# DeltaNet and MLP-mixer on one core: the joins of 16-blocks with block-diagonal operands over the whole array, and a new instruction order

## The chip, the cores and the metric

The kernel runs on one core of a Trainium2 chip. The metric is the device time of one execution in microseconds (us); the kernel before takes 701.34 us, the median of three runs between 700.79 and 702.61. TensorE (PE) does matmuls out of SBUF into PSUM; VectorE (DVE), ScalarE (ACT) and GpSimd (POOL) work element by element; SyncE (SP) issues all the DMAs here. Each engine takes its instructions in the order of its own queue, and waits where an operand isn't there yet.

## The reference

Two blocks follow each other: a delta-rule attention (4 sequences, 8 heads, 768 steps, 48 features) and an MLP-mixer on its output (width 384, token mixing of 256, channel mixing of 1536).

```python
k_n = k / (np.linalg.norm(k, axis=-1, keepdims=True) + 1e-06)
state = np.zeros((B, H, D, D))
for t in range(S):
    kt, vt, bt = k_n[:, :, t], v[:, :, t], beta[:, :, t, None]
    y[:, :, t] = np.einsum('bhd,bhde->bhe', q[:, :, t], state)
    v_old = np.einsum('bhde,bhd->bhe', state, kt)
    state = state + bt[:, :, :, None] * np.einsum('bhd,bhe->bhde', kt, vt - v_old)

x = y.transpose(0, 2, 1, 3).reshape(B, S, H * D)
h = np.maximum(x.transpose(0, 2, 1) @ w_tok1, 0.0) @ w_tok2
u = x + h.transpose(0, 2, 1)
out = u + np.maximum(u @ w_ch1, 0.0) @ w_ch2
```

All arithmetic is float32; the four weight matrices come in as float64 and are rounded to float32 on the chip.

## The kernel before

**Units.** A sequence is cut into 12 chunks of 64 steps; two neighbouring chunks of all 8 heads are a *unit* of 128 steps, so a sequence has 6 units and the batch 24. Unit u's keys and queries are loaded (`load_kq`, job k), transposed and multiplied with one another (`prep`, job p). That yields for every chunk and head a strictly triangular 64x64 matrix, whose entries couple a step to the earlier ones. Its inverse (of the identity plus it) turns the step-by-step rule into a few matmuls per chunk. Both lie in the array `gm`: 8 pairs (`nb`) along the free dimension, 128 partitions.

**The inverse, in blocks.** A 64x64 block is cut into 32x32 diagonal blocks, four per unit and `nb` (`quarters`). The diagonal blocks are inverted by VectorE for a whole *round* of units at once (`invert`, job i), with one block per partition, by repeated multiply (L553) and add (L558). Rounds hold units 0 to 3, 4 and 5, then four units each. The blocks get there and back in two ways:

- The first batch (units 0 to 5, rounds 0 and 1) stays in SBUF: four copies per unit (`to_parts`, L501), a VectorE transpose (L545), and four copies back (`from_parts`, L520). The four copies go to ScalarE, VectorE, ScalarE and GpSimd. Here only the 16x16 halves of each 32-block are inverted on VectorE, and `join_16` (job h, L579 on) makes the off-diagonal 16x16 part of each 32-block: p_z = block x its second inverted half (transposed in `t16`), L587; a scaled copy of it into `z16`, L591; p_x = z x block, L599; four copies into the block. `low16` is 1 on the rows of the second half of each 32-block and 0 elsewhere.
- The later units go through DRAM (`n_dram`, `w_dram`) and have all 32 columns inverted on VectorE, in 30 steps.

`join` (job j) then makes the 32x32 part of each 64-block in the same way: a VectorE transpose into `t11` (L614), p_z (L619), copies into `zst`, p_x (L628), copies back.

In the 16-block join every matmul works on a 32x32 tile of TensorE, four tiles for each of the 8 `nb`:

```python
for nb in range(NB):
    for i, (block, _, _) in enumerate(quarters(u)):
        r = slice(HB * i, HB * i + HB)
        nc.tensor.matmul(p_z[r, nb], block[:, nb], t16[r, :, j * NB + nb])
```

**The recurrence.** Job r walks the chunks of all heads, each step needing the state of the step before: p_k or p_q, p_w, p_s and, in the first batch (`recur_early`), p_y, with copies and subtractions on ScalarE and VectorE between. A recurrence step of unit u needs that unit's join. After the 12 chunks of a batch, `mixer` (job m) does token mixing (p_1, L887; p_h, L900) and channel mixing (p_ut, L910; p_c, L973; p_o, L992) and stores the output. The last pair of rows of the last batch stores its second row block in two halves (L1023, L1031).

**Weights.** 34 pieces are loaded as 64-bit words and rounded (`round_weights`, job w), on ScalarE, VectorE and GpSimd. Pieces w22 to w33 are those of `wc2` (`round_pair`); w24 and w25 lie in its second block `wc2[:, 1]`.

**The order.** Nothing is scheduled while the kernel runs or is built: every job is a Python generator that issues some instructions and yields. A string of words, 2,142 steps long, says which job is advanced when, and with it the order of every engine's queue:

```python
for word in order.split():
    name, _, n = word.partition("*")
    for _ in range(int(n or 1)):
        next(jobs[name])
```

Words x, z and Y issue matmuls on zeros whose result isn't used (`keep_warm` with one or four banks, `warm_tiles`); m0 to m3 are the mixers.

Of the kernel before, what the change touches and what calls it, by code (L numbers as in the profile page):

```python
# [13 lines left out]
C = 64  # L14
U = 128
DP = 64
HB = 32
QB = 16
# [5 lines left out]
def kernel(  # L24
# [70 lines left out]
    def ps_prep(shape, name):  # L95
        return psum.tile(shape, FP32, name=name, tag="prep", bufs=2)
# [176 lines left out]
    def round_pair(j, src):  # L273

        m, k = divmod(j, 2)
        b = wc2[:, m]
        yield from round_weights(
            b[:, 2 * k : 2 * k + 2].rearrange("p j n -> p (j n)"), src, (id(wc2), j)
        )
        if k == 0:  # L280
            return
        assert (id(wc2), j - 1) in rounded
        for out, x, y in ((4, 1, 0), (1, 3, 1), (5, 3, 4), (6, 2, 5)):
            nc.vector.tensor_tensor(
                out=b[:, out], in0=b[:, x], in1=b[:, y], op=ALU.subtract
            )
            rounded.add((id(wc2), m, "sum", out))
            if out != 4:
                yield
# [19 lines left out]
    joined_16 = set()  # L309
    joined = set()  # L310
# [153 lines left out]
    z16 = spare[:, cuts[2] : cuts[3]].rearrange("s (b t) -> s b t", t=QB)  # L464
# [30 lines left out]
    def to_parts(u):  # L495
        rnd, j = round_of[u]
        if u < NCH:
            t = turned_of(rnd)
            for i, (block, at_t, _) in enumerate(quarters(u)):
                on = (nc.scalar.copy, nc.vector.tensor_copy, nc.scalar.copy, nc.gpsimd.tensor_copy)[i]  # L500
# [13 lines left out]
    def from_parts(u):  # L514
        rnd, j = round_of[u]
        assert rnd in turned_back
        if u < NCH:
            for i, (block, at_t, _) in enumerate(quarters(u)):
                on = (nc.scalar.copy, nc.vector.tensor_copy, nc.scalar.copy, nc.gpsimd.tensor_copy)[i]
# [57 lines left out]
    def join_16(u):  # L577
# [17 lines left out]
        for nb in range(NB):
            for i, (block, _, _) in enumerate(quarters(u)):
                r = slice(HB * i, HB * i + HB)
                nc.tensor.matmul(
                    p_x[HB * i : HB * i + QB, nb], z[r, nb], block[:, nb, QB:HB]  # L599
                )  # L600
        yield
        for i, (block, _, _) in enumerate(quarters(u)):
            on = nc.vector.tensor_copy if i in EARLY_DVE else nc.scalar.copy
            on(out=block[0:QB, :, QB:HB], in_=p_x[HB * i : HB * i + QB])
# [275 lines left out]
    def mixer(b):  # L880
# [39 lines left out]
        def store(c, e=slice(0, DM)):  # L920
            nc.sync.dma_start(out=out[b, c * 128 : (c + 1) * 128, e], in_=xb[:, c, e])
# [21 lines left out]
        for c in range(0, NCH, 2):  # L943
# [77 lines left out]
            final = (b, c) == (B - 1, NCH - 2)  # L1021
            if final:
                store(c + 1, slice(DH, DM))  # L1023
# [7 lines left out]
            store(c + 1, slice(0, DH) if final else slice(0, DM))  # L1031
# [33 lines left out]
    w10 z x*2 w10*2 k0 x z b w2 w1 k0 w10 k0*3 w10 k0 x p0 w2*2 p0 b*2 p0 x k1 w2 w1  # L1065
    p0*3 w2 k2 p0 w1 k3 p0*2 k1 z p0*2 z k1*2 p0 w3 k2 k1*2 p1*2 p0 v0*2 k2 k4*2 k2
    p1*2 k2*2 p1*6 k3 p2 w3 k3*2 p2 k3*2 k4*3 w3 p1*3 p2*3 p3*2 k6 p2 k5 p2*3 p3*3
    p2*4 p0 p4*2 k5 p3*3 p1 p3*3 w1*2 p3 p2 p3 p1 p2*2 p0 p4 k4 p0 w3 p2 p3*3 p1*2
    p4*2 p3 p0 k6*2 z w6 k6*2 p4*4 x i0 w3 i0 k6 w18 k5*4 p4 i0*3 w6 i0 w18 i0 p5
    i0*4 v0 p4*2 i0*3 w18 i0*2 p4*2 w18 w6 w13 k8 p5 i0 h0*2 p6 h1 k8 h1 w6 p5 w6  # L1070
    f0*2 v0 v1 v0 p4 k7*2 f1 k7 f1*2 f0*2 f1 w13 h2*2 h0 k7*3 z p6 w18 w13 p6 h0*4
    p7 j0*2 w8*2 h1 p5 w13*2 w8 f2*3 j0 h1*3 p7 w8 h1 Y j1 p6 w11*2 w8 w11 j0 p5 j0
    p5*4 r0*2 w17 f2 w17 h2*2 r0 h2*3 w11 v1 w17 p7 p4*2 p5 r0 p5*3 v1*2 r1*2 k8 r0
    Y w17*2 p5 w11 w14*2 r1 k8 r1 h3 p5*3 r1*2 r0 f3*2 j1*2 h3 f3 i1 r1*2 f3 v1 i1
    k9*4 w0 v2*4 p6 w14 r2 i1 j2 p6*5 j1*2 r2 r1 i1 p7 r2*3 w0 j2*2 i1 w14 w0 r2 i1
    h3*2 r2*2 w0 v2 h3*3 k9 k8 k9 i1 r3*2 k10 i1*2 p6*2 j3 i1 k8 p6 r3 w0 r3*2 j2
    r3*3 w14 p7 p8 p7 j2 p7 k10*2 r4*2 i1 v3 w9*2 p7*3 r4*3 i1 j3*2 v3 w9*2 r4 j3 i1
    j3 r4 w5*2 r2 r5 p6 r4*2 p6*2 w9 i1 p8 p6 k10*2 r5 w5*2 i1 p7*3 k11 v3 r5*3 p8*2
    w5 k10 k11 r5*3 p8*2 i1 p8*2 r5 v3*2 w16 v4 w16 r6*3 w16 w24*2 i1 w27 v4 p7 v4
    p7 h5*2 r6*2 w16 h4 w16 p7 r6*2 p8*2 w27 v4 w24 p9 h4 f4*4 r6*2 r7*2 p9 w24 w27  # L1080
    p9 p10 w24 p8 w27 p8*2 w27 r7*4 f5 p7 k12 w28*2 p9*7 w28 r7*3 v5*2 h4*4 w26 z
    w29 h4 p8 p9 v5*2 w26 f5*2 w26 f5 p9*2 r3 v4 w26 h5*2 z j4 h5*3 w28 k13 p8 w26
    w29 p8 j4*2 w29 r8 p8 w28 w29 k12 j4 v5 p9*2 j4 j5 r8 z p9 r8 p10*3 r8*2 p9 j5
    w7*3 w29 r8*3 i2*3 p10 j5*3 w7 r9*2 w15*2 i2 r9*3 k13 w7 w15*2 i2 r9*4 k12*2 w4
    i2 k12 w4 i2 r8 w4 w15 p12 r10*2 i2*2 w19*2 p10 k11*2 r10*4 i2 w19 v6 w4*2 k11*2
    r10*2 i2 w19*2 w22 k12 i2 r10 r11*3 m0 i2 r11*2 w22 i2 v6 m0 w12 k13*2 w12 i2
    w22 w31 i2 v6 i2*2 w12 i2*3 w12 v7 k13 v7*3 r11*2 i2*2 w12 i2 w21 w22*2 i2 w25
    i2 v6*2 i2*6 m0*2 p10*5 f6 m0*3 p12 m0 f6 m0 w27 m0*2 p10 m0 f6*2 w31 m0*2 f8
    w21*2 r12 v7 w21 Y w31 j6 w21 f7*3 w20 f7 f8*2 j6 w25*2 p10 j7 j6 w25*3 p11*2
    w20*2 f8 w23 w31 w27 w20 w31 w27 w20 m0*2 j7 j6*2 w23*2 p11 p12 m0 p10*3 j8 m0*2  # L1090
    f9*3 p10 k13 r12*2 w23*2 j7 m0 r12*2 j8 m0 j7*2 r13*2 m0 w23 p11 p12 p13 j8
    w32*2 p11 r13*2 w32 p11 m0 p13 r13*2 p13 w32*2 p11*4 m0 r14*2 p11 m0 w29*2 v8*2
    r14 w30 p11*2 j8 w23 w25 r14 p12 w30*2 r14 w23 r14 m0 w30 j8 w30 w25 k14 r15*2
    p13 p12 p11 p12*3 m0 v8*2 p12 v8 r15*2 p12 m0*2 w33*2 f9 p11*2 r15 p12*2 r15 w33
    m0 w29 p13*5 m0 p11 v9 w33 r16*2 j9 k14*4 k15 p12*4 p13*2 v9*2 p13*6 w33*2 m0*2
    w33*2 w31 v9 w31 j9 r16 p14*2 m0*3 r16*3 j9 p14 m0 w31 p14*2 r17*2 m0 v9 j9*2
    k14 i3 r17*2 i3*2 m0 i3 k15 v10 p14*4 k15 v10 i3 v10 i3 k16 v10 i3 k15*2 m0*2
    i3*2 r17*2 m0*2 r18 k15 i3*4 m0*3 i3 p14 r18 i3*3 k16*3 m0 i3*2 k16*2 i3*13
    r18*2 p15 p14*2 m0 p14*2 r18*2 m0*5 f10 v10 m0*7 f10*3 m0 r19 f11*2 r19 p14 p15
    f11 j10 m0 p15 m0*3 r19*2 j10*2 f13*4 f12 p15*2 m0 r19*2 j10 m0 p15 p16 f12 r20  # L1100
    v11 p14 f11 j10 p15*4 r20 m0 j11 f12 r20*2 k17*2 p15*2 k17 v11 f12 v11*3 p14
    p15*2 m0 p15 r20 p15 r20 j11 j12 m0 r21 j11*3 r21 j12 r21*2 m0 s*2 p16*5 j12 p16
    k17*2 v12 k18 m0 v12 m0 p17 j13 r21*2 p16*3 m0 r22 p17 r22 k18 k17 p17 v12 p16*4
    m0 s p17 r22*2 m0 r22 p16 r22 p16*2 m0 r23*2 p17*2 p15 m0*2 v13 m0*2 r23 p17*2
    m0 r23 v12 r23 v12 r23 k19 p17*3 m0*3 v13*2 k18*4 p17*5 m0*2 p17 j13 m0 j12 i4*2
    m0*3 i4*3 m0 i4 m0 i4 v13 m0*2 i4*2 k19 m0*2 k19*2 i4*2 m0 i4 p18 i4 m0*3 k19
    i4*2 j12 j13 m0 k19 j13 i4*2 r24*2 m1 i4 r24*3 m1*2 i4 r25 i4*2 p18*2 r25 i4*3
    v14*2 i4 j13 m1 i4 m1 r25 v13 m1 r25*3 m1 p18 r26*2 i4 m1 v14 i4 v14 i4 p18 i4
    p18 k20 r26 m1 i4*2 r26*3 m1 p19 v14 p18*4 m1 f14 s r27*2 p18*3 f14*2 k20*2 m1*3
    r27*2 p19*2 m1*2 j14 f15*2 f14 f16 f15*2 m1 r27*2 j14*2 m1*2 j15 r28*2 j14 f16  # L1110
    j14 j15*2 k20 f16 p18*2 m1 f17*2 k20 r28*2 p19 j16 m1 p20 r28 j16 r28 j15*2
    r29*2 p20 j16 m1 p19*4 r29 p19 k20 m1 p20 r29*2 p19 v15 p19 f17 r29 v15*4 m1*2
    r30*2 p18 f16 m1*4 r30*2 v16 k21 v16 p18 k21 p19 k21*3 p19 p21 m1 p21 m1*2 v16
    r30 v16*2 p20*4 r30 p20*3 m1 p21 k21 p19*3 r31*2 p20*2 k22*3 p20*3 f17 p20 m1*2
    k22 j16 k22 r31 m1*3 j16 r31 j17 m1 r31*2 v17*2 p20 p21*2 v17 p21*3 m1 r32*2 m1
    p21 m1*2 r32*2 p21 p19 k22 v17 p22 p21*3 p22*2 m1 r32*2 m1 p21*4 p22*2 m1*2
    r33*2 m1 j17 r33*2 k23 m1 k23 i5*3 v17 m1*2 i5*4 v18 k23*2 v18*3 r33 k23*2 r33
    p22 j17*3 i5 m1 p23 m1*3 i5*2 m1 i5 m1 i5 r34 i5*2 m1 r34 m1*7 r34*2 m1 i5 p22
    m1*4 i5 r34*2 m1 i5 m1 i5 m1*2 v18 p22 i5*3 m1*5 r35 m1*6 i5*3 m1*3 i5*2 m1 i5*2
    m1*2 i5*4 p23*2 m1 f18*3 r35 m1 f19 m1 p22*2 f19 f20 f19 f20*3 m1*2 r35*2 p22*3  # L1120
    m1*2 p23 j18 p23 p22*2 m1 p23 f18 m1*5 j18*2 m1*3 p23 m1*2 r35 j19*2 j18 p22 f19
    m1 v19*3 j19 m1*2 p22 m1*6 f21*4 m1*2 j18 m1 p23 m1*2 v19 m1*6 r35 r36*2 p23*4
    r36*3 m2 p23 j20 r37 j20 j19 v19 p23 r37*3 p23*3 v20 m2 j21 r37*2 j20 m2 v20 r38
# [45 lines left out]
```

## Time and profile before

| what | value |
|---|---|
| median of three runs | 701.34 us |
| the profiled execution, its own time | 703.88 us |
| its span, first to last instruction | 702.1 us |
| TensorE busy | 660.9 us (94%) |
| VectorE busy | 476.5 us (68%) |
| ScalarE busy | 279.7 us (40%) |
| GpSimd busy | 105.9 us (15%) |
| mean granted TensorE clock | 0.944 of full speed |

The profile is of one execution. Its page has the engines' busy time, the span in 40 slices, the DMA queues, the chain that ended last (followed back from the last instruction, at each step to what released it), and the costliest groups of instructions. A group is named by the line of the code, the engine, and output<-inputs. The granted clock is the speed at which TensorE was allowed to run, as a share of full speed. Ends of matmuls are modelled, so "busy" on PE is not PE at its peak. Every float32 matmul of the code shows as two instructions in the counts.

### The profile page before, as it was taken

Reading aid. Unit: us, or ns where it says so; the run is one execution under the profiler, and the core shown is the slowest. Engines: PE = TensorE matmul, PEld = TensorE weight load, DVE = VectorE, ACT = ScalarE, POOL = GpSimd, SP = SyncE. Lnnn points to the kernel's source line nnn. Section 1 sums busy time; section 2 is a strip of 40 time slices with the busy share of each in tenths; the row PEclk is TensorE's granted clock in tenths of the full one; section 3 lists DMA queues with packets and bytes.
Section 4 is the critical chain, followed back from the end, with each engine's and each line's share of the span. In section 5 each row is a group of like instructions: output and inputs, shape, how many; then the busy total and the mean of one; then the engine's idle time right before and its main releaser. Section 6 shows DMA issues by size and latency. Waiting matters only on the chain.

```text
span 702.1 us, 18867 instructions
## 1 busy us (share of the span) xinstructions
PE 660.9 (94%) x7794; PEld 594.8 (85%) x7794; DVE 476.5 (68%) x1263; ACT 279.7 (40%) x659; POOL 105.9 (15%) x130
## 2 busy tenths in 40 slices
PE   8448988798999999999999999999999999999998
PEld 5337885656999999987999999977999996999998
DVE  6998787898899955499577895358955533252433
ACT  7647476424642233312743414233424231142230
POOL 2336234225231011101112000000000000000000
PEclk9856689599999999999999999999999999999999
DMA  9844656635254233412444104020020000000000
GB/s 183 168 91 112 112 142 149 166 85 110 65 95 111 60 63 74 86 38 62 76 70 94 41 1 95 8 56 15 13 54 14 1 23 1 22 2 23 1 23 23
DMA packets 146901, 46.15 MB, mean 66 GB/s; under 512 B 138080, under 2 KB 141280, under 8 KB 146816
## 3 DMA queue, kind: packets, MB, share of 16 engines
q1 hardware_dynamic: 146816, 44.95, 29.9%
q8 instruction: 61, 1.00, 0.6%
q14 instruction: 24, 0.20, 0.1%
HBM read 35.49 MB, written 9.44 MB: 64 GB/s over the span
## 4 chain that ended last, share of the span: by engine, by line
PE 83%; DVE 11%; DMA 2%; issue 2%; ACT 2%; SPq 0%; ACTq 0%; DVEq 0%
PE p_o L992 24%; PE p_r L818 7%; PE p_c L973 7%; PE p_c L818 7%; PE p_d L818 5%; PE p_q L730 4%; PE p_s L756 4%; PE p_w L746 4%; PE p_h L900 3%; PE p L887 3%; PE p_g L436 3%; PE p_z L619 2%; PE p_x L628 2%; DVE sub L553 2%; DVE x L558 2%
## 5 line engine op out<-in xcount | busy, mean ns | idle before, releaser
L992 PE MATMUL p_o<-wc,r 128*128 128x192 f32 x720 | 126.0, 328 | 0.6 <-ACT u_t L914 0.6
L992 PEld LDWEIGHTS p_o<-wc,r 128*128 128x128 f32 x720 | 116.4, 190 | 1.8 <-ACT u_t L914 1.1
L918 DVE TENSOR_TENSOR xb<-xb,p_o 128x192 f32<-128x192 f32 x84 | 29.5, 352 | 57.0 <-PE p_o L992 56.6
L558 DVE TENSOR_TENSOR x<-x,sub 128x84 f32<-128x84 f32 (+24 forms) x178 | 59.8, 336 | 6.1
L553 DVE TENSOR_TENSOR sub<-x 128x84 f32<-128x84 f32 (+24 forms) x178 | 58.1, 326 | 7.6 <-DMA x<-n_dram 3.9
L973 PE MATMUL p_c<-u_t,wc 128*128 128x256 f32 x216 | 52.1, 392 | 0.0
L835 DVE TENSOR_TENSOR r<-p_r,r 128x384 f32<-128x384 f32 x36 | 20.0, 555 | 46.1 <-ACT r L864 35.6
L992 PE MATMUL p_o<-wc,s 128*128 128x192 f32 x288 | 50.7, 327 | 0.0
L264 POOL TENSOR_TENSOR w_f<-w_f,d 128x384 uint32<-128x384 uint32 (+1 forms) x34 | 34.2, 1008 | 94.9 <-DVE w_f L257 50.1
L838 ACT ACTIVATE r<-r 128x384 f32<-128x384 f32 x72 | 37.5, 524 | 23.6 <-DVE r L835 21.5
L992 PEld LDWEIGHTS p_o<-wc,s 128*128 128x128 f32 x288 | 46.8, 190 | 0.0
L749 ACT COPY rw_bd<-p_w 64x192 f32<-64x192 f32 x72 | 22.4, 311 | 59.1 <-PE p_w L746 53.6
L973 PEld LDWEIGHTS p_c<-u_t,wc 128*128 128x128 f32 x216 | 40.6, 194 | 5.8 <-issue 0.7
L818 PE MATMUL p_r<-u_t,wc 128*128 128x128 f32 x324 | 45.4, 276 | 0.0
L818 PE MATMUL p_c<-u_t,wc 128*128 128x128 f32 x324 | 45.2, 276 | 0.0
L358 POOL TENSOR_TENSOR v_st<-v_st,nrm 128x384 f32<-128x384 f32 x24 | 20.2, 845 | 165.3 <-DMA v_st<-in_v_dram 116.4
L818 PEld LDWEIGHTS p_r<-u_t,wc 128*128 128x128 f32 x324 | 40.8, 192 | 0.1
L818 PEld LDWEIGHTS p_c<-u_t,wc 128*128 128x128 f32 x324 | 40.5, 192 | 0.2 <-issue 0.2
L415 POOL TENSOR_TENSOR mb<-mask_c,cs 128x512 f32<-128x512 f32 x20 | 21.2, 1059 | 128.9 <-DVE cs L397 113.2
L436 PE MATMUL p_g<-kqt 64*64 64x128 f32 x704 | 29.4, 299 | 7.4 <-ACT kqt L425 5.9
L887 PE MATMUL p<-xb,w 128*128 128x384 f32 x96 | 35.5, 509 | 0.0
L730 PEld LDWEIGHTS p_q<-s_bd,kqt 128*128 128x128 f32 x264 | 33.3, 192 | 2.1 <-issue 0.5
(185 smaller groups left out, 1283.4 us busy)
## 6 DMA issues: line engine op xcount, KB each, us to landing
d<-in_moe_w_ch_dram SPq DMA_DIRECT2D x24, 384.0 KB, 3.7
v_st<-in_v_dram SPq DMA_DIRECT2D x96, 48.0 KB, 2.7
out_dram<-xb SPq DMA_DIRECT2D x23, 192.0 KB, 1.9
kpad<-in_k_dram SPq DMA_DIRECT2D x18, 192.0 KB, 3.9
qpad<-in_q_dram SPq DMA_DIRECT2D x18, 192.0 KB, 3.6
kst<-in_k_dram SPq DMA_DIRECT2D x64, 48.0 KB, 2.9
n_dram<-gm SPq DMA_DIRECT2D x72, 32.0 KB, 1.9
gm<-w_dram SPq DMA_DIRECT2D x72, 32.0 KB, 2.0
```

Of the source, the lines that this page charges most:

```text
L264: nc.gpsimd.tensor_tensor(out=f, in0=f, in1=lo, op=ALU.add)
L436: nc.tensor.matmul(p_g[cc][PAR[i ^ cc], p], kqt[PAR[i], 2 * p + cc, 0], kqt[PAR[i], 2 * p + cc],)
L553: nc.vector.tensor_tensor(out=tmp, in0=y[:, :, 0:s, s : s + 1].to_broadcast([n, k, s, w]), in1=y[:, :, s : s + 1, s + 1 : m].to_broadcast( ...
L558: nc.vector.tensor_tensor(out=y[:, :, 0:s, s + 1 : m], in0=y[:, :, 0:s, s + 1 : m], in1=tmp, op=ALU.add,)
L730: nc.tensor.matmul(p_q[:, p], kqt[:, 2 * p + cc], s0[:, p])
L746: nc.tensor.matmul(p_w[0 : C + 1, p], gm[:, 2 * p + cc, 0 : C + 1], r_bd[:, p])
L818: nc.tensor.matmul(p[:, i], weight(g * n + i), b_, start=first and i == 0, stop=True, skip_group_check=True,)
L838: nc.scalar.activation(out, out, ACTF.Relu)
L887: nc.tensor.matmul(p_1[dh], piece_of(w1, c, 0)[:, dh * 128 : (dh + 1) * 128], xb[:, c], start=(c == 0), stop=(c == NCH - 1),)
L918: nc.vector.tensor_tensor(out=xb[:, c, e], in0=xb[:, c, e], in1=p, op=ALU.add)
L973: nc.tensor.matmul(p_c[:, k], piece_of(wc1, cb, f * 128)[:, f * 128 : (f + 1) * 128], u_t[:, cb], start=(cb == 0), stop=(cb == NCB - 1),)
L992: nc.tensor.matmul(p, a[:, m], wc2[:, m, j], start=(start and m == 0), stop=(m == NM - 1), skip_group_check=True,)
```

## The change

- **Operands.** `z16` goes. Two zeroed operands come: `t16_bd` in its place (128 x 512) and `z16_bd` (128 x 1024), which lies in `wc2[:, 1]` until the weights come there. Both are zeroed by GpSimd. An assertion holds the rounding of w24 and w25 back until all six units have used them.
- **join_16.** Four ScalarE copies put the unit's four 16-column blocks of `t16` on a block diagonal. p_z is then one matmul per `nb` with the unit's whole 128 x 64 stationary operand, and 64 moving columns. Four scaled activations, in place of one, put its diagonal blocks into `z16_bd`. p_x is one matmul per `nb` with 128 stationary and 32 moving columns. The final four copies stay.
- **Block copies.** In `to_parts` and `from_parts` the fourth copy goes from GpSimd to VectorE; `EARLY_DVE` is (1, 3).
- **Last store.** The output's last row block is stored in one piece.
- **Order.** The string of words is new throughout. Each job h has 8 words in place of 7; z, x and Y occur 17, 11 and 2 times in place of 9, 6 and 3.

```diff
@@ round_pair
-        yield from round_weights(
+        late = range(NCH) if m == 1 else ()
+        for n, _ in enumerate(round_weights(
             b[:, 2 * k : 2 * k + 2].rearrange("p j n -> p (j n)"), src, (id(wc2), j)
-        )
+        )):
+            yield
+            assert n != 3 or used_16.issuperset(late)
@@ operands
     t16 = spare[:, cuts[1] : cuts[2]].rearrange("s (t b) -> s t b", t=QB)
-    z16 = spare[:, cuts[2] : cuts[3]].rearrange("s (b t) -> s b t", t=QB)
+    t16_bd = spare[:, cuts[2] : cuts[3]].rearrange("s (b i t) -> s b i t", i=4, t=QB)
+    z16_bd = wc2[:, 1].rearrange("s j n -> s (j n)")[:, 0 : NB * 4 * HB].rearrange(
+        "s (b i t) -> s b i t", i=4, t=HB
+    )
+    for t_ in (t16_bd, z16_bd):
+        nc.gpsimd.memset(t_, 0.0)
@@ to_parts and from_parts, the same line in both
-                on = (nc.scalar.copy, nc.vector.tensor_copy, nc.scalar.copy, nc.gpsimd.tensor_copy)[i]
+                on = nc.vector.tensor_copy if i in EARLY_DVE else nc.scalar.copy
@@ join_16
-        z = z16[:, bs]
-        p_z = ps_prep([128, NB, QB], "p_z")
+        wt = gm_of(u)
+        rows = [slice(HB * i, HB * i + HB) for i in range(4)]
+        for i, r in enumerate(rows):
+            nc.scalar.copy(t16_bd[r, :, i], t16[r, :, bs].rearrange("s t b -> s b t"))
+        yield
+        taken_16.add(u)
+        p_z = ps_prep([128, NB, 4 * QB], "p_z")
         for nb in range(NB):
-            for i, (block, _, _) in enumerate(quarters(u)):
-                r = slice(HB * i, HB * i + HB)
-                nc.tensor.matmul(p_z[r, nb], block[:, nb], t16[r, :, j * NB + nb])
-        taken_16.add(u)
-        yield
-        nc.scalar.activation(z, p_z, ACTF.Copy, scale=low16)
+            nc.tensor.matmul(
+                p_z[0:C, nb], wt[:, nb, 0:C], t16_bd[:, nb].rearrange("s i t -> s (i t)")
+            )
+        yield
+        for i, r in enumerate(rows):
+            r2 = rows[i % 2]
+            nc.scalar.activation(
+                z16_bd[r, :, i, 0:QB], p_z[r2, :, QB * i : QB * i + QB],
+                ACTF.Copy, scale=low16[r2],
+            )
         yield
         assert inverted.issuperset((u, i) for i in range(4))
-        p_x = ps_prep([128, NB, QB], "p_x")
+        p_x = ps_prep([128, NB, 2, QB], "p_x")
         for nb in range(NB):
-            for i, (block, _, _) in enumerate(quarters(u)):
-                r = slice(HB * i, HB * i + HB)
-                nc.tensor.matmul(
-                    p_x[HB * i : HB * i + QB, nb], z[r, nb], block[:, nb, QB:HB]
-                )
+            nc.tensor.matmul(
+                p_x[:, nb], z16_bd[:, nb].rearrange("s i t -> s (i t)"),
+                wt[:, nb, 0:C].rearrange("s (two t) -> s two t", two=2)[:, :, QB:HB],
+            )
+        used_16.add(u)
         yield
         for i, (block, _, _) in enumerate(quarters(u)):
             on = nc.vector.tensor_copy if i in EARLY_DVE else nc.scalar.copy
-            on(out=block[0:QB, :, QB:HB], in_=p_x[HB * i : HB * i + QB])
+            on(out=block[0:QB, :, QB:HB], in_=p_x[HB * i : HB * i + QB, :, i % 2])
@@ mixer, the last stores
-            final = (b, c) == (B - 1, NCH - 2)
-            if final:
-                store(c + 1, slice(DH, DM))
...
-            store(c + 1, slice(0, DH) if final else slice(0, DM))
+            store(c + 1)
@@ the order: all lines replaced; here those around the third inversion's end
-    i2 v6*2 i2*6 m0*2 p10*5 f6 m0*3 p12 m0 f6 m0 w27 m0*2 p10 m0 f6*2 w31 m0*2 f8
-    w21*2 r12 v7 w21 Y w31 j6 w21 f7*3 w20 f7 f8*2 j6 w25*2 p10 j7 j6 w25*3 p11*2
-    w20*2 f8 w23 w31 w27 w20 w31 w27 w20 m0*2 j7 j6*2 w23*2 p11 p12 m0 p10*3 j8 m0*2
+    v6*3 i2 k11 w12 k13 v6 w31*2 i2*2 w24*2 i2*2 w24 i2*3 w31 p10*4 r11 m0*2 p10 r11
+    w24 x w24 w31*2 w12*2 m0*3 v6 p12 p10 w25 w12*2 w21 r12 w25*2 z f6*3 p12*2 p10
+    w20 f6 w25 j6*2 w25 p11 w21*2 z j6 f7*3 w20 w21 j6*2 j7 w20 j7*2 w21 p11 w20
+    w23*3 r12*2 w23 p11 w20 f9 w23 p11*2 p12*2 r12 w29 m0 r12 m0*2 p11 m0 w25 w23*2
```

## The prediction

> **What bounds the kernel now.** I read the page first: engine busy times, the slices, the chain by line. Then busy time by stage, the chain in order of time, and the engines' timelines where a stage changes hands.
>
> ```profile
> PE 660.9 (94%) x7794; PEld 594.8 (85%) x7794; DVE 476.5 (68%) x1263; ACT 279.7 (40%) x659; POOL 105.9 (15%) x130
> PEclk9856689599999999999999999999999999999999
> ```
>
> Averaged, TensorE is the bound; the clock digits say that the first quarter is another regime. Busy time by stage (columns: busy us and instructions of PE, weight load, VectorE, ScalarE, GpSimd, then granted clock, DMA share, GB/s) shows where it ends:
>
> ```profile
> 29.30:42.40 13.10, 1.99 (x32) 1.58 (x32) 12.28 (x39) 1.68 (x4) 3.30 (x4) 0.51 0.72 131
> 56.60:98.00 41.40, 37.55 (x993) 33.80 (x992) 32.66 (x92) 23.50 (x60) 15.72 (x18) 0.71 0.56 115
> 125.40:156.60 31.20, 27.16 (x264) 18.45 (x264) 29.00 (x85) 11.40 (x27) 6.02 (x8) 0.73 0.47 114
> 164.30:698.50 534.20, 533.54 (x5132) 497.00 (x5133) 337.64 (x886) 186.36 (x434) 47.51 (x54) 1.00 0.21 45
> ```
>
> From 164.3 us on PE idles 0.7 us in 534: the end is "when the saturated part begins" plus "what PE still has to do then". Before it, VectorE bounds the first and second inversions and the third one (125.4 to 156.6), and PE, largely at half clock, the recurrence steps between. The chain in order of time (start, duration, step) shows the hand-over:
>
> ```profile
> 115.65 2.98 DMA n_dram<-gm
> 118.82 6.61 DMA x<-n_dram
> ...
> 156.41 0.21 DVE x L558
> ```
>
> PE's timeline there (start, duration, group, in brackets the idle time before it and its releaser):
>
> ```profile
> 152.14 4.48 PE L900 MATMUL p_h<-r,w 128*128 128x384 f32 x12
> 157.15 4.14 PE L900 MATMUL p_h<-r,w 128*128 128x384 f32 x12 [0.52 <-DVE xb L904]
> 161.12 0.82 PE L910 MATMUL p_ut<-ident,xb 128*128 128x128 f32 x6
> 164.35 0.69 PE L619 MATMUL p_z<-t,gm 32*32 32x32 f32 x32 [1.82 <-DVE t L614]
> ```
>
> The last unit of the third inversion is sent out at 115, its 30 steps run on VectorE to 156.6, its result goes through DRAM, and the join of unit 6 (p_z of L619) starts at 164.35. While it waits for that, PE does p_h and p_ut of the first mixer.
>
> **What the skill says.** The Trainium skill, "TensorE: Matmul & The Clock Gate", Part 2 (Step-by-step): weight-load time scales with the columns, not the rows. The trace agrees: 8 passes (four matmuls, two records each) of p_s (112 columns) hold PE 0.77 us and 8 of p_q (128 columns) 0.87 us in the chain, 0.096 and 0.109 us a pass at the same 96 moving columns. The Trainium skill, "TensorEngine Tiling (Array Packing)", The Solution: 32x32 tiles run independently. Agrees: the 64 passes of a p_z of the 16-block join take 0.66 us (98.06 to the next group at 98.72), 10 ns each. The Trainium skill, "TensorE: Matmul & The Clock Gate", Part 1: the clock is halved until PE has been busy for a window of about 3.4 us. The trace shows halved stretches (0.51 in the table's first row) but also 0.5 from 77 to 94 us with PE busy on small tiles, so busy time alone doesn't lift it. The Trainium skill, "GPSIMD Engine Reference", section 8, Key points: GpSimd shares its SBUF interfaces with VectorE and can contend with it. Agrees: the VectorE copy of L501 takes 367 ns alone and 858 beside a GpSimd copy.
>
> **The change, part by part.** Six units, each with one 16-block join. Queue positions are those of the two built programs.
>
> *PE, the joins.* Removed per unit: 64 passes of p_z (0.62 us by cadence) and 64 of p_x (0.62). Added: 8 matmuls, 16 passes, for p_z with 64 columns and 64 moving; at the 0.87 ns per column of the rows above 0.056 us, so 0.90 us. And 16 passes of p_x with 128 weight columns: 0.112 us like p_q, so 1.79. Net +1.45, six units +8.7 us, at full clock, all before 164 us. Bounds: if a pass with 32 moving columns went at p_w's 0.083 us, p_x is 1.33 and the net is +1.0; at half clock both double. I take +8.7.
>
> *ScalarE.* Added: four copies into the block-diagonal operand (128 elements, strided; half of L501's strided 256, whose 0.63 us lie on about 0.19 fixed, gives 0.41) and four scaled activations in place of one (L591 takes 0.358 for 128 elements; the Trainium skill, "ScalarE: Activation LUTs", section What ACT_TABLE_LOAD costs, gives 186 + 93 + 0.833 x 128 = 386 ns for such a one, an estimate). 4 x 0.41 + 3 x 0.36 = 2.7 us, six units +16 us. ScalarE is 78 us busy in the first 122, so most of it finds room. Not all: between the transposed 16-blocks (42.3) and the first p_w (56.7, 14.4 us) ScalarE's new queue holds 18.1 us of work, about 15.5 if neighbours overlap by 0.09 us each: +1 us there, and zst, rw_bd and all of unit 0's join stand behind it.
>
> *VectorE.* The fourth of every four block copies, in both directions, moves from GpSimd: 12 copies at 0.37 us, 4.4 us (0.86 if still beside GpSimd: 10). Summing each queued instruction's median duration up to the gm write of the last unit of the third round (113.6 us): 101.0 before, 106.1 in the new queue. Up to the end of the third inversion: 138.6, then 142.7, so +4.1. Against it, about 1 us: the two copies stretched to 0.86 had a GpSimd copy beside them, which is gone.
>
> *GpSimd.* 12 copies fewer (8 us), which nobody waited long for. Two memsets more (128x512 took 0.53 at L479; 128x1024 about 1.0) stand ahead of the first w_f, before which GpSimd idles 3.05 us: free. The second operand lies in wc2's second block, so pieces 24 and 25 are rounded after the last join. Their first user, p_o, stands 44 us of PE work behind the join of unit 6: free; late pieces would stop PE at p_o.
>
> *Warm-ups.* 9 to 17 four-bank and 6 to 11 one-bank ones, 3 to 2 tile sets: +7.8 us of PE at full clock. They stand where PE idles (12 of them between unit 4's first transposes and the first p_w), cost nothing there, and may lift the clock: PE's path from 76.7 to 94.3 ran at half clock, 17.6 us for 8.8 us of work. VectorE idled only about 5 us there, which caps the gain. I take half, -2.6, for 0 to -5.
>
> *Order.* In the new PE queue p_z of unit 6 stands ahead of the first mixer's p_h and p_ut. PE issues in order: p_x, unit 7's join and the next p_w stand behind that p_z, p_h behind them too, and the wait that p_h covered now covers only warm-ups. Summing the PE queue by cadence from that p_z to the end: 526.5 us before, 535.8 now, **+9.3**: 12 p_h of two passes at 0.323 (7.75), 6 p_ut at 0.109 (0.65), one four-bank warm-up (0.87). This is the main term. It falls away only if unit 6's join comes correspondingly earlier.
>
> *SP's queue.* 439 issues for 440. Of the moved ones, the third inversion's x load is issue 116 instead of 118, behind the same four n_dram stores and one v_st load more; its w_dram store is 140 instead of 147. Both wait for VectorE's results, which the sum above dates; I add nothing. If the v_st load held its buffer's wait there, the x load would be late by that wait, in the range above.
>
> *Tail.* The last store is whole: 192 KB land in 1.9 us, 96 KB in 1.6: +0.3; one issue less on SP, ahead of nothing.
>
> **Sum.** Start of the saturated part: +4.1 - 1.0 - 2.6 = +0.5, with ScalarE's +1 inside the error. PE work left there +9.3, tail +0.3, together +10.1. I shade it by 1.5 because VectorE idled 17.8 us of the 156.4 and a new order may fill some of that: +8.6. The profiled execution (703.9 us around a span of 702.1) would become 712.5; it lies 2.5 us above the median of the runs, 701.3, which becomes 710.
>
> **Rivals.**
> *The clock pays (faster).* Mechanism: whole-array matmuls and more warm-ups keep PE at full clock from 42 to 98 us. For it: clock 0.50 and 0.71 there, and PE on the chain from 51 to 58 and from 77 to 97. Price: half of 6.6 + 17.6 us, 12 us; it decides once unit 6's join starts more than 9.6 us earlier, before 154.7 us. Against: VectorE's queue holds 4 us more and was 89% busy. 698.
> *Absorbed.* The new order uses VectorE's idle time and the join starts some 6 us earlier: 701.3 + 9.6 - 7 = 704. For it: gaps of 0.3 to 2.3 us in VectorE's timeline. Against: these wait for PE, which has more to do.
> *All of it lands.* PE's +8.7 and ScalarE's +16 are met on the recurrence's path; the join starts 8 us later: 719. For it: PE fills 37.6 of 41.4 us there. Against: PE's chain is rarely the last to end after 98.
> *Not what it says.* If a pass takes its 32 moving columns, not its weights, the joins cost nothing more; the order term stays: 708, within the main case.
>
> **From cases to numbers.** Main case 0.57 (704.5 to 715); all lands 0.14 (715 to 722); absorbed 0.19 (699.2 to 704.5); clock pays 0.10 (below 699.2). A measurement of this kernel can tell about 0.3%, 2.1 us: of "absorbed" 0.11 lie below 703.4 and count as the same. Slower 0.79, same 0.11, faster 0.10. Leaving out the clock case and the upper part of "all lands" gives 700 to 717.
>
> **What the new profile would show.** Right: p_h after p_z of unit 6 and after that unit's first p_w; PE idle or on warm-ups just before that p_z; it starts within 4 us of 164.4; p_x of the 16-blocks near 1.8 us per unit at full clock; PE idle near nothing afterwards. Wrong: that p_z before 158 (clock or gaps), after 170 (the joins are on the path), or idle PE after it (a wait that I haven't priced, first of all for pieces 24 and 25).

## The result, and the profile after

The changed kernel is slower: 723.02 us (median of four runs, 718.93 to 728.78) against 701.74 for the kernel before (four runs), a ratio of 1.0311 with a 95% interval of 1.0274 to 1.0347. That is outside the stated range (700 to 717); the direction was forecast. The page of the profiled execution, itself the longest of the four (728.78 us, span 727.0):

```profile
PE 685.9 (94%) x7236; PEld 614.2 (84%) x7236; DVE 476.5 (66%) x1275; ACT 295.3 (41%) x701; POOL 97.9 (13%) x120
PEclk9755799586899999999999999999999999999999
```

Busy time per engine over the whole span says little: TensorE +25 us, ScalarE +16, VectorE the same. The table by stage, with this kernel's own stage limits (columns as before: PE, weight load, VectorE, ScalarE, GpSimd, granted clock, DMA share, GB/s):

```profile
29.30:41.90 12.60, 4.96 (x36) 3.08 (x37) 9.37 (x38) 2.67 (x6) 0.32 (x1) 0.50 0.83 182
41.90:68.10 26.20, 23.89 (x163) 17.64 (x162) 16.34 (x41) 19.74 (x49) 7.96 (x9) 0.57 0.37 90
136.40:169.60 33.20, 23.43 (x329) 16.60 (x328) 28.01 (x82) 9.47 (x24) 7.25 (x10) 0.71 0.33 81
177.90:727.00 549.10, 544.78 (x5166) 504.31 (x5166) 340.47 (x893) 187.27 (x436) 45.85 (x53) 0.99 0.21 45
```

The kernel before, for the second and the last of these stretches:

```profile
41.60:56.60 15.00, 11.38 (x402) 8.79 (x402) 13.64 (x33) 11.97 (x30) 7.03 (x8) 0.50 0.35 91
164.30:702.10 537.80, 534.17 (x5134) 497.33 (x5134) 338.00 (x887) 186.36 (x434) 47.51 (x54) 1.00 0.21 45
```

Two rows of the changed kernel carry the loss. The second is the stretch from the first inversion's transposed 16-blocks to the first p_w: 26.2 us, 15 before. PE is busy in 23.9 of them, VectorE in only 16.3 (before: PE 11.4, VectorE 13.6 of 15). Half clock alone isn't the difference, since the stretch ran at 0.50 before too. The last row is the saturated part, from unit 6's p_z to the end: 549.1 us, 537.8 before. The chain in order of time shows what fills the first of these (start, duration, step):

```profile
46.79 1.97 PE p_z L600 x16
48.76 2.01 PE p_warm L200 x2
50.77 3.25 PE p_x L614 x16
54.02 1.87 PE p_warm L200 x2
...
56.74 3.25 PE p_x L614 x16
...
64.47 3.71 PE p_warm L200 x4
68.18 1.02 PE p_w L694 x16
...
168.41 0.83 DVE sub L562
...
177.44 0.36 DVE t L632
...
177.93 0.69 PE p_z L637 x31
```

The whole-array joins and the warm-ups stand one behind the other on PE, at half clock (p_x takes 3.25 us for its 16 passes), and the recurrence's first p_w behind them. PE's timeline after the join of unit 6 shows the order that was forecast, p_h and p_ut behind that p_z:

```profile
177.93 0.69 PE L637 MATMUL p_z<-t,gm 32*32 32x32 f32 x32 [2.18 <-DVE t L632]
...
186.23 5.35 PE L918 MATMUL p_h<-r,w 128*128 128x384 f32 x16
...
192.28 2.77 PE L918 MATMUL p_h<-r,w 128*128 128x384 f32 x8
194.89 0.82 PE L928 MATMUL p_ut<-ident,xb 128*128 128x128 f32 x6
```

One trace of this kernel isn't enough, since its runs lie 10 us apart. A second one, of a run of 721.97 us, is taken below.

### The profile page after: what moved, and what is told of

Same layout as the page of the kernel before. It is cut to its first block, busy times and chain, and to the rows that moved or that the text cites. A ratio compares the mean times of both kernels' runs of the same rounds, so it can differ in the third digit from the quotient of the medians.

```text
span 727.0 us, 17803 instructions
## 1 busy us (share of the span) xinstructions
PE 685.9 (94%) x7236; PEld 614.2 (84%) x7236; DVE 476.5 (66%) x1275; ACT 295.3 (41%) x701; POOL 97.9 (13%) x120
## 4 chain that ended last, share of the span: by engine, by line
PE 86%; DVE 5%; ACT 4%; DMA 3%; issue 2%; POOL 1%; SPq 0%; POOLq 0%; ACTq 0%
PE p_o L1010 23%; PE p_r L836 7%; PE p_c L836 7%; PE p_c L991 7%; PE p_d L836 5%; PE p_h L918 4%; PE p_s L774 4%; PE p_q L748 4%; PE p_w L764 4%; PE p L905 3%; PE p_warm L200 2%; PE p_g L440 2%; PE p_x L646 2%; PE p_z L637 2%; PE p_x L614 2%
## 5 line engine op out<-in xcount | busy, mean ns | idle before, releaser
L567 DVE TENSOR_TENSOR x<-x,sub 128x84 f32<-128x84 f32 (+24 forms) x178 | 57.5, 323 | 6.1
L991 PE MATMUL p_c<-u_t,wc 128*128 128x256 f32 x216 | 50.5, 383 | 0.0
L440 PEld LDWEIGHTS p_g<-kqt 64*64 64x64 f32 x704 | 22.8, 148 | 27.4 <-ACT kqt L429 25.1
```

Source lines behind the costliest of these rows:

```text
L440: nc.tensor.matmul(p_g[cc][PAR[i ^ cc], p], kqt[PAR[i], 2 * p + cc, 0], kqt[PAR[i], 2 * p + cc],)
L567: nc.vector.tensor_tensor(out=y[:, :, 0:s, s + 1 : m], in0=y[:, :, 0:s, s + 1 : m], in1=tmp, op=ALU.add,)
L991: nc.tensor.matmul(p_c[:, k], piece_of(wc1, cb, f * 128)[:, f * 128 : (f + 1) * 128], u_t[:, cb], start=(cb == 0), stop=(cb == NCB - 1),)
```

## The experiments

All times are medians of four runs or more; the kernel before ran beside each group and took 701.1, 702.9, 701.5 and 702.0 us there. "First p_w", "p_z" (unit 6's) and "rest" (from that p_z to the end of the span) come from one trace each.

A trace is of one run, and the runs of one kernel differ. Five of these traces have the same code and the same order up to the end of the third inversion on VectorE (before; to p_1; to p_z; mixer shifted; transpose earlier), and it ends there at 156.7, 152.4, 159.1, 152.0 and 152.7 us. So a difference of a few us in "first p_w" or "p_z" between two traces shows nothing; the medians and the rest are steadier.

| kernel | time | first p_w | p_z | rest |
|---|---|---|---|---|
| before | 701.7 | 56.7 | 164.4 | 537.8 |
| changed, first trace | 723.0 | 68.1 | 177.9 | 549.1 |
| changed, again | 723.3 | 63.5 | 171.2 | 549.0 |
| changed, six warm-ups out | 724.3 | 62.3 | 171.7 | 550.8 |
| changed, tile joins | 717.2 | 58.7 | 162.0 | 550.5 |
| changed, tile joins, six warm-ups out | 718.9 | 56.6 | 167.7 | 550.6 |
| changed, p_x in tiles | 719.9 | 64.4 | 169.2 | 549.7 |
| changed, copies shared | 724.6 | 68.0 | 177.7 | 549.0 |
| changed, p_h moved ahead by hand | 730.5 | 63.6 | 181.6 | 547.1 |
| changed to the third inversion, tile joins, then before's order | 710.4 | 58.9 | 170.1 | 538.3 |
| before to p_1, then changed order | 712.1 | 55.2 | 160.0 | 549.2 |
| before to p_z, then changed order | 716.3 | 55.4 | 170.9 | 546.1 |
| before, mixer shifted by eight words | 739.5 | 55.2 | 158.1 | 578.9 |
| before, whole-array joins one by one | 738.7 | 74.5 | 199.0 | 538.8 |
| before, copies only | 704.0 | 56.0 | 164.3 | 538.3 |
| before, unit 6's transpose earlier | 700.7 | 56.2 | 158.8 | 539.4 |

### The changed kernel again

No edit.

> The changed kernel once more, for a second trace of it. In the first one the clock was 0.939 and the time the longest of four (728.8). If the stretch from 42 to 68 us at half clock is the rule, the first p_w again stands at 66 to 69 us; if it was that run's bad luck, a run near the median of 723 has it at 60 to 64, as in the kernel without warm-ups (62.3).

Measured: 723.33 us, ratio 1.0315 (1.0239 to 1.0391); in the traced run (721.97) the first p_w at 63.5, p_z at 171.2, rest 549.0. So part of the first trace's stretch was that run's clock. Granted clock in steps of 4 us from 48 us on, first trace:

```profile
48.00:52.00 4.00, 4.00 (x18) 2.85 (x16) 2.43 (x9) 3.70 (x9) 0.00 (x0) 0.50 0.61 155
52.00:56.00 4.00, 4.00 (x14) 2.86 (x14) 1.05 (x3) 1.78 (x6) 1.10 (x1) 0.50 0.34 98
```

and second trace:

```profile
48.00:52.00 4.00, 4.00 (x20) 2.50 (x20) 3.06 (x10) 3.37 (x9) 0.47 (x1) 0.82 0.39 75
52.00:56.00 4.00, 3.56 (x55) 3.03 (x53) 1.62 (x5) 3.84 (x11) 1.55 (x2) 1.00 0.35 98
```

The same instructions run at half clock in one run and at 0.82 to 1.00 in the other; the first p_x takes 3.25 us there and 1.72 here. The rest differs by 0.1 us. From here on the second trace is the one to compare with: start +6.9 us, rest +11.2. Together that is 18.1, and the medians differ by 21.6: the trace of before is of a run 2.2 us above its median, this one of a run 1.4 below. By the medians the start is some 10 us later.

From the transposed 16-blocks to the first p_w:

```profile
40.90:63.50 22.60, 17.58 (x160) 12.81 (x160) 17.47 (x40) 19.47 (x48) 8.30 (x9) 0.77 0.40 101
```

Summed over the pieces of the chain in this stretch, PE holds 11.8 us of it (5.4 of them warm-ups), ScalarE 9.1 (4.5 of them copies into `t16_bd`), VectorE 0.6. Before it was VectorE 7.9, PE 5.5, ScalarE 1.0.

### Warm-ups taken out

```diff
-    w18 h0 x h1 f0 w18 h1 h0 p5 p6 f0*3 z p6 k8*2
+    w18 h0 h1 f0 w18 h1 h0 p5 p6 f0*3 p6 k8*2
...
```

(two x and four z in all, between unit 0's first p_z and the first p_w)

> The changed kernel without the six warm-up words (x and z) that stand between unit 0's first p_z and the first p_w. Theory 'PE's path': those matmuls took 8.2 us of PE's unbroken chain from 46.8 to 68.1 us at half clock, so the first p_w comes at 59 to 62 us instead of 68.1, p_z of unit 6 some 6 to 8 us earlier than 177.9, and the time is about 716 against 723. Rival 'the warm-ups pay by the clock': without them the half clock lasts longer, and the time stays at 723 or rises. Rival 'ScalarE and VectorE set it': the first p_w moves by less than 3 us, and so does the end.

Measured: 724.25 (723.06 to 724.32), first p_w 62.3, p_z 171.7. Against the first trace that looks like 6 us gained; against the second it is nothing, and the time is the same as with them. In this trace the clock stays at half from 48 to 72 us. The mean granted clock of the four runs is 0.941 to 0.943; of the eight runs with the warm-ups seven have 0.947 to 0.964 and one 0.939. So the warm-ups go with a higher clock in most runs, and still gain no time. The theory "PE's path" falls as far as these six go; that they pay isn't shown either.

### Tile joins in the new order

```diff
-        for i, r in enumerate(rows):
-            nc.scalar.copy(t16_bd[r, :, i], t16[r, :, bs].rearrange("s t b -> s b t"))
         yield
...
-            nc.tensor.matmul(
-                p_z[0:C, nb], wt[:, nb, 0:C], t16_bd[:, nb].rearrange("s i t -> s (i t)")
-            )
+            for i, (block, _, _) in enumerate(quarters(u)):
+                r = slice(HB * i, HB * i + HB)
+                nc.tensor.matmul(p_z[r, nb], block[:, nb], t16[r, :, j * NB + nb])
```

(the scaled activation and p_x likewise as before)

> The changed kernel, its order and its warm-ups, but with the 16-block joins as 32x32 tiles as before (an empty step stands where the block-diagonal copies were). Theory 'whole-array joins at half clock': 10.4 us of p_z and p_x in the chain from 46.8 to 68.1 shrink to about 4.5, and the eight ScalarE copies ahead of the second p_z (4.4 us) go; the first p_w comes 6 to 9 us earlier than 68.1, the time is 714 to 717. Rival 'warm-ups and order alone': the first p_w moves by less than 3 us, the time is 720 or more.

Measured: 717.18 (714.33 to 718.27), ratio to before 1.0205 (1.0144 to 1.0266). The joins' form costs 6 us in this order (7.5 by the ratios to the kernel before that ran alongside). In its trace the first p_w is 4.8 us earlier than in the second one above, p_z 9.3. Its table by stage:

```profile
41.90:58.70 16.80, 13.32 (x402) 8.00 (x402) 15.49 (x35) 11.92 (x28) 8.20 (x9) 0.80 0.41 104
162.00:712.50 550.50, 545.74 (x5166) 504.63 (x5166) 341.54 (x893) 187.18 (x436) 46.30 (x53) 0.99 0.21 45
```

VectorE is again busy in 15.5 of 16.8 us. The rest is still 12.7 us longer, so the two terms are separate. The start (162.0 against 164.4) looks earlier than before, but this is the fastest of four runs: by the medians, 15.5 us slower with 12.7 in the rest, it is still some 3 us late.

Without the six warm-ups as well:

> Tile joins and, besides, none of the six warm-up words between the first p_z and the first p_w; otherwise the changed kernel. With tile joins and warm-ups it took 717.2, with whole-array joins and no warm-ups 724.3. Theory 'the joins' form costs, the warm-ups don't matter': 717 again, first p_w at 56 to 59. Rival 'the warm-ups pay by the clock once PE has room': the clock stays at half to 65 us and beyond, and the time is 720 or more. Rival 'they cost on the path': 712 to 714.

Measured: 718.94 (715.78 to 720.08). Within the spread of the runs above: the first expectation holds, and these six warm-ups are neutral with tile joins too. The clock was lower without them, as the rival said (0.929 to 0.933 in four runs, 0.936 to 0.954 with them), but the time did not reach its 720.

### What of the joins costs

p_x alone as tiles, out of the diagonal blocks of the same operand:

```diff
-            nc.tensor.matmul(
-                p_x[:, nb], z16_bd[:, nb].rearrange("s i t -> s (i t)"),
-                wt[:, nb, 0:C].rearrange("s (two t) -> s two t", two=2)[:, :, QB:HB],
-            )
+            for i, (block, _, _) in enumerate(quarters(u)):
+                r = slice(HB * i, HB * i + HB)
+                nc.tensor.matmul(
+                    p_x[HB * i : HB * i + QB, nb, i % 2], z16_bd[r, nb, i, 0:QB], block[:, nb, QB:HB]
+                )
```

> The changed kernel with p_x alone as 32x32 tiles, read out of the diagonal blocks of the same operand (p_z, the copies and the scaled activations as changed). If p_x's passes with 128 stationary columns carry the join's 6 us (they take 1.8 us a unit at full clock and 3.3 to 3.6 at half, tiles 0.6 to 1.4): 717 to 720, first p_w 3 us or more earlier than 63.1. If the ScalarE work and the waiting of one unit for another carry it: 722 to 725.

Two of four copies into `t16_bd` on VectorE:

```diff
-            nc.scalar.copy(t16_bd[r, :, i], t16[r, :, bs].rearrange("s t b -> s b t"))
+            on = nc.vector.tensor_copy if i in EARLY_DVE else nc.scalar.copy
+            on(out=t16_bd[r, :, i], in_=t16[r, :, bs].rearrange("s t b -> s b t"))
```

> The changed kernel with two of each unit's four copies into the first block-diagonal operand on VectorE, not ScalarE. With tile joins the changed kernel takes 6 us less; this asks whether ScalarE's copies carry that. If they do: the first p_w 2 us or more earlier than 63.1, the time 719 to 721. If they don't: 722 to 725.

Measured: 719.93 (718.81 to 720.69) with p_x in tiles, 724.57 (722.51 to 728.52) with the copies shared. About 3.3 of the 6 us go with p_x's passes, by the times. That the first p_w would come 3 us earlier failed (64.4; a load's landing holds 3.1 us of the chain in that trace), so where on the way the gain lies is not shown. Sharing the copies gains nothing; VectorE has two of the four instead, so that doesn't clear them. The other 2.7 us (p_z's form, the scaled activations) are not split further.

### Whole-array joins in the old order

The first try put the new `join_16` into the kernel before as it stands, the second operand in `wc2[:, 0]`. It computes something else: units 1 and 2 overwrite the operand before unit 0's p_x has read it, since there is room for one unit.

> The kernel before with one part of the change alone: the 16-block joins with block-diagonal operands over the whole array (the second operand lies in the first block of wc2; copies, order and store as before; the copies into the block diagonal go with p_z in one step). Theory 'whole-array joins at half clock': the first p_w comes 5 to 8 us later than 56.7, the time is 706 to 710. Forecast's own sum for this part: PE +8.7 us at full clock, mostly beside VectorE, and ScalarE +1: the first p_w at most 2 us later, the time 701 to 704.

Measured: 739.42, first p_w at 77.3. The second moved the words of units 1, 2 and 5 behind the p_x of the unit before:

```diff
-    h0*2 p6 h1 k8 h1 w6 p5 w6 f0*2 v0 v1 v0 p4 k7*2 f1 k7 f1*2 f0*2 f1 w13 h2*2 h0
+    h0*2 p6 k8 w6 p5 w6 f0*2 v0 v1 v0 p4 k7*3 f0*2 h0 h1*2 f1*4 w13
...
```

> The kernel before with the whole-array joins alone, one unit after the other, since the operands have room for one unit only: words of units 1, 2 and 5 move behind the p_x of the unit before (operands in the first block of wc2; copies, store and the rest of the order as before). Theory 'whole-array joins cost at half clock, and by waiting for one another': the first p_w 6 us or more later than 56.7, the time 708 to 720. Forecast's sum for this part: the first p_w at most 2 us later, 701 to 704.

Measured: 738.66 (736.27 to 739.62), ratio 1.0521 (1.0454 to 1.0587). First p_w at 74.5, 18 us late; p_z at 199.0; rest 538.8, as before. PE's timeline:

```profile
44.09 1.97 PE L595 MATMUL p_z<-r,wc 128*64 128x64 f32 x16 [15.08 <-ACT r L591]
49.95 3.59 PE L609 MATMUL p_x<-wc 128*128 128x32 f32 x16 [3.90 <-DVE r L506]
...
60.93 1.06 PE L631 MATMUL p_z<-t,wc 32*32 32x32 f32 x32 [3.48 <-ACT d L251]
61.92 3.62 PE L609 MATMUL p_x<-wc 128*128 128x32 f32 x16
```

Here PE idles as well: each unit's p_z, scaled activations and p_x run after the p_x of the unit before. Larger than either expectation. An explanation would be that operands with room for one unit put the six joins in single file, where `z16` had room for four units. That is argued, not shown: in the first try three units' p_z go ahead of unit 0's p_x, and it took as long. What both share is the whole-array form, four more ScalarE copies and three more scaled activations a unit, in an order made for tiles. With the new order the form costs 6 us instead of 37.

### The copies alone

```diff
-                on = (nc.scalar.copy, nc.vector.tensor_copy, nc.scalar.copy, nc.gpsimd.tensor_copy)[i]
+                on = nc.vector.tensor_copy if i in EARLY_DVE else nc.scalar.copy
```

> The kernel before with one part alone: in both directions the fourth block copy on VectorE, not GpSimd. Forecast's terms for it: +4.1 us of VectorE's queue less 1.0 us of contention, of which idle VectorE takes some: 701 to 705. Rival 'GpSimd beside VectorE costs more than the copies': 697 to 700.

Measured over 20 runs: 704.01, ratio 1.0031 (1.0010 to 1.0051), 2.2 us. VectorE's extra copies cost about what was forecast.

### p_h and the order

By hand, in the changed kernel: p_h, p_ut and unit 10's p_g ahead of unit 6's p_z, weight piece 25 behind it.

```diff
-    w24 x w24 w31*2 w12*2 m0*3 v6 p12 p10 w25 w12*2 w21 r12 w25*2 z f6*3 p12*2 p10
-    w20 f6 w25 j6*2 w25 p11
+    w24 x w24 w31*2 w12*2 m0*3 v6 p12 w25 w12*2 w21 m0*8 p10 r12 z f6*3 p12*2 w20 f6
+    j6*2 w25*3 p10*2 w25 p11
...
```

> The changed kernel with the first mixer's p_h and p_ut (and one p_g of unit 10) ahead of unit 6's p_z, as before; the rounding of weight piece 25 moves behind that p_z. Theory 'order': PE idles 9.2 us between 157.7 and 166.9 there, so p_h finds room; p_z of unit 6 starts at most 2 us later than 177.9, what PE does from it on shrinks from 549 to about 540, and the time is 714 to 717 against 723. Rival 'PE is full there anyway': p_z of unit 6 starts 6 us or more later, and the time is 721 or more.

Measured: 730.53 (729.02 to 733.47), slower by 7, p_z at 181.6. VectorE's timeline shows why (in brackets the idle time before):

```profile
172.06 0.55 DVE L922 TENSOR_TENSOR xb<-xb,p_h 128x384 f32<-128x384 f32 x1 [2.32 <-PE p_h L918]
173.54 0.56 DVE L922 TENSOR_TENSOR xb<-xb,p_h 128x384 f32<-128x384 f32 x1 [0.93 <-PE p_h L918]
...
179.64 0.43 DVE L632 STREAM_TRANSPOSE t<-gm 128x256 f32<-128x256 f32 x1
...
192.15 0.73 DVE L787 COPY s_bd<-p_s 48x192 f32<-48x192 f32 x2
```

VectorE's six additions of p_h wait for PE one by one; unit 6's transpose and the roundings stand behind them, and then r12's `s_bd` behind the roundings. PE, which has the 7.7 us less to do (busy 537.1 after p_z, 544.8 in the changed kernel), idles 10 us instead. My expectation had priced PE's queue and not VectorE's.

The opposite, in the kernel before: the mixer from its first p_h on eight words later.

```diff
-    m0*2 p10*5 f6 m0*3 p12 m0 f6 m0 w27 m0*2 p10 m0 f6*2 w31 m0*2 f8
+    m0*2 p10*5 f6 m0*2 p12 f6 w27 p10 f6*2 w31 f8
...
```

> The kernel before, with the first mixer's steps from its first p_h on eight places later in the order, so that p_h and p_ut stand behind unit 6's p_z, as in the changed kernel (the rounding of weight piece 23 moves behind p_h, because the two share buffers). Theory 'order': unit 6's p_z starts 0 to 3 us before 164.4, and PE has 9 us more to do from there: 707 to 711. Rival 'PE's order there is free': 700 to 703.

Measured: 739.54 (738.81 to 740.28). Both expectations missed, and inconclusive on p_h alone: the shift upset the whole first mixer. What PE waited for after p_z (us, times, longest):

```profile
PE p_o L992 <- DVE xb L918: 10.9, 4, 7.8
...
PE p_h L900 <- ACT r L895: 6.7, 1, 6.7
PE p_q L730 <- DVE s_bd L769: 1.7, 1, 1.7
```

So two whole orders were joined instead: one kernel's words up to a place, then the other's remaining words. The kernel before (tile joins, its copies), changed order from the first mixer's second p_1 on, so p_h late:

```diff
-    i2 v6*2 i2*6 m0*2 p10*5 f6 m0*3 p12 m0 f6 m0 w27 m0*2 p10 m0 f6*2 w31 m0*2 f8
+    i2 v6*2 i2*6 k13 w31*2 p10*4 m0 p10 w31*2 m0*3 p10 r12 w25*2 z f6*3 p12*2 p10
...
```

> The same with the changed order's words from the first mixer's second product on, so that p_h and p_ut stand behind unit 6's p_z, as in the changed kernel. Theory 'order of p_h': the part from unit 6's p_z on is 547 to 551 us, as in all four kernels with the new order (549.0 to 550.8), p_z starts 0 to 3 us before 164.4, and the time is 706 to 712, 6 to 9 above the kernel that changes order only from that p_z on. Rival 'PE's order is free': no difference between the two.

The converse, the changed kernel with tile joins up to the middle of the third inversion and then the old order, so p_h early:

```diff
-    i2*4 w19 i2*2 v6*3 i2 k11 w12 k13 v6 w31*2 i2*2 w24*2 i2*2 w24 i2*3 w31 p10*4
+    i2*4 w19 i2*2 v6*2 w24 p12 k11*2 k12 m0 w24*2 w12*2 w31 w24 v6 w12*2 w24 v7*4
...
+    i2*6 m0*2 p10*5 f6 m0*3 p12 m0 f6 m0 w27 m0*2 p10 m0 f6*2 w31 m0*2 f8
...
```

> The converse: the changed kernel with tile joins, its own order up to the middle of the third inversion, and from there the remaining words in the order of before, so that p_h and p_ut stand ahead of unit 6's p_z. Theory 'order of p_h': the part from that p_z on falls from 550.6 to about 538 to 541, p_z stays at 162 to 168, and the time is 701 to 708 against 717.2. Rival 'the new order is slow elsewhere, or p_h ahead only delays p_z, as in the try with words moved by hand': 715 or more.

Measured: 712.07 (709.87 to 716.68), ratio 1.0143 (1.0082 to 1.0205), and 710.38 (709.16 to 711.97), 6.8 below the changed kernel with tile joins. The saturated part of the two, first with p_h late and then, in the second fence, early:

```profile
160.00:709.20 549.20, 545.02 (x5166) 503.81 (x5166) 341.77 (x893) 187.47 (x436) 46.00 (x53) 0.99 0.20 43
```

```profile
170.10:708.40 538.30, 534.35 (x5134) 497.49 (x5134) 337.98 (x887) 186.58 (x434) 47.08 (x54) 1.00 0.21 45
```

That settles the rest: seven kernels with the new order from there on have 549.0 to 550.8, five with the old one 537.8 to 539.4, whatever their joins, copies, warm-ups and start. The instruction counts of PE (5166 and 5134) differ by 32: 24 of p_h, 6 of p_ut and 2 of a warm-up, as forecast. Two things are not settled. The splices exchange nearly all words behind the place, so the gain isn't shown to be p_h's alone. And a shorter rest isn't all gained: in the second splice p_z came at 170.1 (162 to 168 expected; 162.0 with the new order), and the time missed its 701 to 708. In the first, the time is as expected at its upper end, and p_z, 4.4 us before 164.4, is outside its 0 to 3; the third inversion ended 4.3 us earlier there, with the same order.

A third splice, the old order up to unit 6's first join word and the new one from there:

> The kernel before, its own order up to unit 6's first join word (so its first mixer's p_h and p_ut stand ahead of that p_z), and from there on the remaining words in the changed kernel's order. If the changed order loses time only before that point and by p_h: the part from unit 6's p_z to the end is 537 to 541 us, as before (537.8), and the time is 700 to 705. If the later order loses too: 545 to 551, and 708 to 714.

Measured: 716.28 (713.36 to 719.34), rest 546.1. p_h is early here, and it is still slow. VectorE's transpose stands behind more roundings, PE idles 4.9 us ahead of p_z, has half clock in the 10 us after it, and then idles 2.5 us for `s_bd`. The spliced words fit neither queue; it doesn't decide between the theories. That it would lie 6 to 9 us below the first splice failed too; it is 4 above.

### A better version?

In the kernel before PE idles 1.8 us ahead of unit 6's p_z. Five rounding words were moved behind it:

```diff
-    f6*2 w31 m0*2 f8 w21*2 r12 v7 w21 Y w31 j6 w21
+    f6*2 m0*2 f8 r12 v7 Y j6 w31 w21*3 w31 w21
```

> The kernel before with five rounding words of weight pieces 21 and 31 moved behind unit 6's first join words, so that VectorE's transpose for unit 6 does not stand behind four of their instructions (1.6 us). PE idles 1.8 us ahead of that p_z in the kernel before. If that idle time is on the path: p_z 1 to 1.8 us earlier against the end of the third inversion, and 699.5 to 700.5 against 701.5. If not: no difference.

Measured: 700.71 (14 runs), ratio 0.9982 by the 12 within 1.5% of the fastest (0.9953 to 1.0012). From the end of the third inversion to p_z it is 6.2 us instead of 7.7, as expected, but the time can't be told from no change. No version here is shown to beat the kernel before.

## Why the prediction was wrong

**Order of p_h and p_ut, +9.3: right as counted, 2 us short.** The rest grew by 11.2 to 11.3 us. Of it 9.3 were the counted passes (p_h's busy time after p_z grows from 25.3 to 33.8 us, p_ut's from 10.2 to 11.3). Some 1.7 more came from the clock in the first 10 us after p_z: 0.66 of full speed against 0.83 before, that is 3.4 us lost against 1.7.

**Start of the saturated part, +0.5: wrong, and this is the step that failed.** It was +6.9 us in the second trace, +13.6 in the first, some +10 by the medians. The sum worked out PE's +8.7 us of joins and then let them cost nothing, as lying beside VectorE; ScalarE's +16 went in as +1 "inside the error". They do lie on the path. In the kernel before VectorE holds most of the chain from the transposed 16-blocks to the first p_w (7.9 of 15.1 us); in the changed one PE and ScalarE hold 21 of 22.7 (second trace). Tile joins take 6.0 us off the time, and p_x alone as tiles 3.3 of these.

The size was off as well. At full clock the passes were priced well (p_x 1.72 us for 16 passes, 1.79 forecast; p_z 1.08, 0.90 forecast), but its bound "at half clock both double" lets the passes that are saved double with the added ones. They don't: the tile passes of p_x take as long at half clock as at full (last section), those of p_z half as long again. The six joins' passes took 20.7 us in the second trace and 23.5 in the first, by the spacing of their starts, against about 8 for the tiles of before: +13 and +16 us in place of +8.7. How the 6.0 us divide between PE's passes and the ScalarE work beyond p_x's 3.3, and whether the room for one unit matters, stays open.

The rival "all of it lands", with a start 8 us later, was this case, given 14%. Its 719 lacks the clock's loss after p_z, and the measured median lies 1 us above its range. The prediction's own sign for it, unit 6's p_z after 170, came true (171.2 and 177.9).

**Warm-ups, -2.6: not found.** Six of the added ones neither cost nor pay, with whole-array joins (724.3 without, 723.3 with) or tiles (718.9 and 717.2); the others were not tried apart. That they "stand where PE idles" failed: on the chain they took 8.2 us of PE in the first trace (2.0, 1.9, 0.6 and 3.7). That they lift the clock held in most runs, without a gain in time.

**VectorE's copies, +4.1 less 1.0: about right**, 2.2 us alone. The prediction's reading of contention is too smooth: of VectorE's six block copies with a GpSimd copy beside them four took 664 to 858 ns and two 371 and 374, about as long as alone.

**ScalarE, +1:** too little by the second trace's chain, where it holds 9.1 us ahead of the first p_w (1.0 before). Sharing its copies with VectorE gained nothing, so what another place for this work would save is not shown.

**The shade of -1.5 for VectorE's idle time: not found.**

**Tail, +0.3: small, as forecast.** From the last addition's start to the end of the span 3.6 us against 2.9, so +0.7.

**SP's queue and the late pieces 24 and 25, nothing:** no wait of PE in the rest names them.

The medians' difference is some 21.5 us. One way to divide it: the order from p_1 on 10.4 (first splice against before), the joins' form 6.0, copies 2.2, together 18.6; the other 3 are the last store (+0.7 above) and the new order ahead of 160 us, and which of its words cost them is open. The other way round the new order's later part costs 6.8 (717.2 against 710.4) and the earlier part 8.7 with the copies and the last store in it (710.4 against 701.7). So the terms don't add up independently of one another: the order's later part costs 7 to 10 us, depending on the start that it follows.

## What to carry to other kernels

Split such a kernel into "when the saturated part begins" and "what the bound engine still has to do then": the second was the same to 2 us over seven kernels and came within 2 us of a count of passes; the first, summed per engine, was off by 6 to 13. Where work moves to another engine ahead of that point, follow the chain through it and ask which engine's work becomes the last to end, rather than taking what one engine has room for as free. Price PE's passes at the clock that this stretch was granted. And a matmul moved ahead in PE's queue brings its VectorE consumer along: price that queue too.

## What was not expected of the hardware

Small tiles hardly feel the half clock here. In the kernel before, the 64 passes of a p_x on 32x32 tiles take 0.54 us from first to last start at 57.7 us, with 0.50 of full speed granted, and 0.52 at 113.8, with 1.00; p_z's take 0.84 and 0.55 (44.2 and 98.1 us). The 16 whole-array passes of p_x in the changed kernel take 3.3 us at 0.50 and 1.7 to 1.8 at 1.00. So part of what the joins lost is that the tile form was nearly immune to a clock that the whole-array form pays for.

The Trainium skill, "TensorE: Matmul & The Clock Gate", Part 1, has the clock released after some 3.4 us of activity. In the first trace PE shows as busy without a gap from 48 to 64 us, whole-array matmuls and warm-ups among it, at 0.50 of full speed in every 4 us of it. In the second trace 0.82 and 1.00 were granted from 48 to 56, to the same queue. Four runs of one kernel lay between 718.9 and 728.8 us with a mean clock of 0.964 to 0.939, in that order. So "busy" in these profiles doesn't tell whether the clock comes; what decides it was not found.
